# Scores of a local attention from fp16 parts scaled by a power of two, instead of rounded float32 parts; eight pairs in plain float32

## The chip, the core and the metric

The kernel runs on one core of one Trainium2 chip. The metric is the device time of one execution in microseconds (us), median of the runs. TensorE appears as PE (matmul) and PEld (weight load), VectorE as DVE, ScalarE as ACT, GpSimd as POOL; SP is the queue from which every transfer is issued.

## What is computed

There are 8 batches of 8 heads, 512 local positions, 32 global positions and a head dimension of 64. Every local query sees the keys within 32 positions and the 32 global keys; every global query sees all 544 keys. The result, joined over the heads to 4352 rows of 512, goes through a two-layer network with the activation h * tanh(softplus(h)).

```
s_g = scale * np.matmul(q_g, k_all.transpose(0, 1, 3, 2))
out_g = np.matmul(sm(s_g), v_all)
s_ll = np.where(mask, scale * np.matmul(q_l, k_l.T), -1e9)     # mask: |i - j| <= 32
s_lg = scale * np.matmul(q_l, k_g.transpose(0, 1, 3, 2))
out_l = np.matmul(sm(concat([s_lg, s_ll])), concat([v_g, v_l]))
h = x @ w_in
return (h * tanh(softplus(h))) @ w_out      # w_in 512 x 2048, w_out 2048 x 512
```

Queries and keys are drawn as normal numbers with spreads of 0.57 to 0.8. The weights arrive as 64-bit numbers and are turned into float32 bits on the chip.

## The kernel before

**Attention.** The unit is a pair of heads of one batch: 4 pairs in each of 8 batches, 32 pairs. A pair has 4 query tiles of 128 positions. For each tile and head `scores` (L594) makes the masked window of 192 or 224 scores, `row_max` (L611) the maximum on DVE, `expo` (L618) the exponentials on ACT, `p_hi` and `p_lo` (L636, L640) two fp16 parts, `p_turn` (L645) a transposing transfer of these (tile `pt`), and `pv` (L649) twelve small matmuls into `U`. `x_norm`, `x_split` and `x_turn` (L664 to L687) scale the result, part it and transpose it into `xh` and `xl`. The global queries go the same way through `g_scores` to `g_pv` (L690 to L751).

**How the scores are multiplied.** Most pairs use rounded float32 parts (type fp32r): `q_hi` and `k_hi` copy the raw tiles into `qs` and `ks`, `q_lo` and `k_lo` subtract to get the small parts (`kl`, and the upper 64 partitions of `qs`). The 128 rows of a matmul hold both parts of q, so that two matmuls, one on `ks` and one on `kl`, make one score tile: four matmuls in a tile of two heads. The first NPS = 5 pairs (`plain_s`: batch 0 and the first pair of batch 1) take float32 queries and keys as they are, 64 rows for each head, one matmul per head and tile (L601), which TensorE runs in two passes, so that the trace counts two. For g there are 12 matmuls in a pair: eight with 256 columns and four with 32.

**The network.** A step is a block of 256 rows and 256 of the 2048 inner columns: `m1_mm` (L779) makes `h` with two groups of 12 matmuls of 256 columns, `mish` (L828) the activation on ACT, `g_hi` and `g_lo` on DVE two fp16 parts `G`, and `m2_mm` (L848) adds two groups of 6 matmuls of 512 columns to `o`. There are 17 blocks of 8 steps; the last block holds the global rows. Block 0 needs `xh` and `xl` of all four pairs of batch 0, so the first `h` cannot stand before the fourth `x_turn`.

**Weights.** 32 halves of 512 KB are loaded (`w_load`); `w_bits` and `w_sum` (L380 to L395) build the float32 bits on DVE, ACT and POOL; `w_stat` (L397) sums squares on PE (`ws`), `w_norm` (L409) takes a scale from a sum over all partitions on POOL (`partition_all_reduce`), and `w_split` (L432) makes fp16 parts, with the low parts of the last ON_POOL = 3 of the first weight's eight column groups, and of all of the second weight, on POOL.

**What sets the order.** Every instruction is a task of `Plan` (L51) with an estimated duration. A list scheduler, run once while the kernel is built, simulates the five queues and emits the tasks in the order of their simulated starts; the engines then work their queues in that order. Priorities are the place in the code plus LATE_* amounts, or slots worked out from CONV1, RATE1, FIRST1 and the like (L1014 to L1028).

## Time and profile before

| | us |
|---|---|
| median of 3 runs | 1021.27 (1020.48 to 1023.16) |
| the profiled execution | 1018.93 |
| its span, first to last instruction | 1017.1 |
| first `h` matmul starts | 132.0 |
| last attention matmul done | 871.6 |

The share of busy time is an average over three stages: a start of 132 us in which batch 0's attention and the weights are made ready, a long middle in which attention and network are interleaved, and an end in which only the network is left. Idle time of an engine is put down to whatever released it last. Matmuls are pipelined, so that one takes longer from start to end than the next one waits; the chain of waits gives the time by which each group pushed the chain on.

### The profile page before, as it was taken

The numbers are of one execution on the slowest core, as the hardware profiler recorded it, in microseconds if no ns is written. First come the engines' busy times: TensorE is split into PE (matmuls) and PEld (weight loads), VectorE is DVE, ScalarE is ACT, GpSimd is POOL, SyncE is SP. The second block draws the span as 40 slices with busy tenths as digits, with TensorE's granted clock in tenths as the row PEclk, the third lists the DMA queues.
The fourth block names the chain that finished last, engine by engine and source line by source line (L and its number), as shares of the span: only waits on it lengthen the run. The fifth ranks groups of instructions, "written<-read, shape, count | busy, mean of one in ns | idle before, by whom it ended". The sixth has DMA issues, their size and how long they took to land.

```text
span 1017.1 us, 20581 instructions
## 1 busy us (share of the span) xinstructions
PE 925.7 (91%) x7906; PEld 664.6 (65%) x7906; DVE 668.5 (66%) x1704; ACT 680.9 (67%) x1321; POOL 82.2 (8%) x62
## 2 busy tenths in 40 slices
PE   3455696899999999999999999999999999999996
PEld 2233475566776777677777777777777777666663
DVE  6977796887766767776677666767676655322221
ACT  3465566777897788878878888788878888211110
POOL 3725231410000000000000000000000000000000
PEclk9997588999999999999999999999999999999999
DMA  9847982587758664766557665666676544100000
GB/s 333 228 111 175 262 259 63 112 180 189 168 104 180 144 143 113 177 148 143 123 153 161 134 133 129 155 135 141 117 165 127 123 81 77 42 1 22 1 22 21
DMA packets 231802, 134.65 MB, mean 132 GB/s; under 512 B 197528, under 2 KB 209048, under 8 KB 230680
## 3 DMA queue, kind: packets, MB, share of 16 engines
q1 hardware_dynamic: 231704, 133.34, 57.1%
q8 instruction: 62, 1.02, 0.4%
q14 instruction: 36, 0.29, 0.1%
HBM read 63.55 MB, written 8.91 MB: 71 GB/s over the span
## 4 chain that ended last, share of the span: by engine, by line
PE 65%; DVE 12%; DMA 8%; ACT 4%; issue 3%; SPq 1%; POOL 0%; ACTq 0%; DVEq 0%
PE o L856 28%; PE h L788 26%; PE s L608 4%; PE U L659 3%; DMA vraw<-in_vm 3%; DMA pt<-ph 2%; PE g L697 2%; DMA gpt<-gph 2%; PE gu L745 1%; DVE vmx L481 1%; DVE P L614 1%; DVE ph L642 1%; DVE G L309 1%; SPq L296 1%; DVE kl L546 1%
## 5 line engine op out<-in xcount | busy, mean ns | idle before, releaser
L856 PE MATMUL o<-W,G 128*128 128x512 f16 x1632 | 389.8, 379 | 0.3 <-POOL W L445 0.3
L788 PE MATMUL h<-xh,W 128*128 128x256 f16 x2048 | 379.0, 275 | 5.1 <-ACT e L831 5.1
L788 PEld LDWEIGHTS <-W 128*128 128x128 f16 x3264 | 311.2, 98 | 68.6 <-issue 5.3
L788 PE MATMUL h<-xl,W 128*128 128x256 f16 x1024 | 281.0, 274 | 0.0
L856 PEld LDWEIGHTS <-G 128*128 128x128 f16 x1632 | 156.9, 98 | 144.1 <-issue 0.6
L831 ACT ACTIVATE e<-h,c 128x512 f32<-128x512 f32 (+1 forms) x137 | 92.6, 683 | 117.5 <-PE h L788 116.6
L623 ACT ACTIVATE P<-P,nm 128x192 f32<-128x192 f32 (+1 forms) x256 | 117.8, 460 | 41.5 <-DVE nm L614 40.3
L309 DVE TENSOR_SCALAR G<-e,c 128x512 f16<-128x512 f32 x129 | 63.9, 495 | 118.5 <-ACT e L831 118.4
L614 DVE CUSTOM_DVE_ANT_0 P<-s,consts 128x192 f32<-128x192 f32 (+1 forms) x256 | 90.1, 367 | 68.1 <-PE s L608 57.7
L642 DVE SCALAR_TENSOR_TENSOR ph<-P,ph 128x384 f16<-128x384 f32 (+1 forms) x128 | 78.0, 611 | 80.1 <-ACT ph L307 79.3
L844 DVE SCALAR_TENSOR_TENSOR G<-e,c,G 128x512 f16<-128x512 f32 (+1 forms) x137 | 102.0, 745 | 3.4
L831 ACT ACT_TABLE_LOAD x79 | 101.4, 1283 | 1.4
L623 ACT ACT_TABLE_LOAD x74 | 94.9, 1283 | 1.3
L659 PEld LDWEIGHTS <-pt 96*128 96x128 f16 (+1 forms) x1536 | 59.3, 101 | 33.5 <-DMA pt<-ph 26.9
L307 ACT ACTIVATE ph<-P 128x384 f16<-128x384 f32 (+1 forms) x128 | 69.7, 548 | 16.3 <-DMA pt<-ph 13.2
L659 PE MATMUL U<-va,pt 128*128 128x64 f16 (+1 forms) x768 | 59.4, 199 | 19.7 <-DMA pt<-ph 19.7
L608 PE MATMUL s<-ks,qs 128*128 128x192 f32 (+1 forms) x216 | 71.4, 353 | 1.4 <-DVE qs L538 0.9
L659 PE MATMUL U<-vc,pt 96*128 96x64 f16 x768 | 58.7, 198 | 0.0
L718 ACT ACTIVATE gP<-g,gmx 64x288 f32<-64x288 f32 x64 | 30.4, 476 | 37.5 <-DVE gmx L713 37.4
L395 POOL TENSOR_TENSOR W<-W,wr 128x512 int32<-128x512 int32 x32 | 48.8, 1535 | 79.0 <-DVE W L393 40.1
L608 PE MATMUL s<-kl,qs 128*128 128x192 f32 (+1 forms) x216 | 54.2, 274 | 0.0
L405 PE MATMUL ws<-W 128*128 128x128 bf16 x128 | 17.7, 286 | 37.4 <-POOL W L395 37.3
(103 smaller groups left out, 1024.3 us busy)
## 6 DMA issues: line engine op xcount, KB each, us to landing
kraw<-in_kt SPq DMA_DIRECT2D x27, 640.0 KB, 4.7
qraw<-in_qt SPq DMA_DIRECT2D x27, 512.0 KB, 3.8
W<-in_w SPq DMA_DIRECT2D x19, 512.0 KB, 7.1
...
```

What stands on the lines that cost most here:

```text
L307: A.activation(out=dst, in_=src, func=AF.Copy, scale=c)
L309: V.tensor_scalar(dst, src, c, None, ALU.mult)
L395: pl.add(POOL, pool(512), lambda: G.tensor_tensor(f(), f(), X["wr", k], ALU.add), r=[("wr", k)], w=[key])
L608: T.matmul(X[s][:, :w], X[qs][:, h, t * 128:(t + 1) * 128], X[k][:, h, c0:c0 + w], start=(i == 0), stop=(i == 1))
L614: pl.add(DVE, 69 + 1.04 * w, lambda: V.tensor_tensor_reduce(out=X[P][:, h, :w], in0=X[s][:, :w], in1=mask[:, m0:m0 + w], scale=-SCALE, sca ...
L623: pl.add(ACT, 160 + 0.832 * w + 93, lambda: A.activation(out=X[P][:, h, :w], in_=X[P][:, h, :w], func=AF.Exp, bias=X[nm], scale=-1.0, accu ...
L642: pl.add(DVE, dve(n), lambda: V.scalar_tensor_tensor(p_part(X[ph], t, 1), p_src(X[P], t), PSC, p_part(X[ph], t, 0), ALU.mult, ALU.subtract ...
L659: T.matmul(X[u][:, t, h, :], X[pt][:k, p * 4 + h * 2 + c, :], X[vx][:k, t, vl, h * 64:(h + 1) * 64], start=(n == 0), stop=(n == 5))
L788: T.matmul(X[h][:, f * TB:(f + 1) * TB], wh(i, wl)[:, off:off + 128], X[x][:, d, o:o + TB], start=(n == 0), stop=(n == 11))
L831: chain(blk, i, ACT, 571, lambda a, z: A.activation(out=X[e][:, a:z], in_=hv(blk, i)[:, a:z], func=AF.Mish, bias=0.0, scale=X[c][:, 0:1]), ...
L844: chain(blk, i, DVE, 602, lambda a, z: V.scalar_tensor_tensor(gp(1, blk, i)[:, a:z], X[e][:, a:z], X["c", blk][:, 2:3], gp(0, blk, i)[:, a ...
L856: T.matmul(X[o], gp(g, blk, i)[:, f, t * 128:(t + 1) * 128], wh(8 + i, wl)[:, f * 512:(f + 1) * 512], start=(i == 0 and n == 0), stop=(i = ...
```

## The change

Eight pairs (batches 0 and 1) now take plain float32 (NPS = 8), in tiles of their own (`qn`, `kn`). For the 24 pairs of batches 2 to 7, queries and keys are first multiplied by powers of two, s and 1/s, which leaves the product as it is, and the parts are fp16. The factor of a batch comes from a new function, `b_norm`: four loads of 544 KB each bring all its queries and keys once more, laid out flat (`mxs`), a reduction of each on DVE takes the largest magnitude, POOL takes it over the partitions, and nine small DVE operations make s and 1/s (`sk`). `q_hi`, `q_lo`, `k_hi`, `k_lo` and `g_split` then multiply by `sk` as they convert. The raw-weight ring `wr` shrinks from two tiles to one, ON_POOL goes from 3 to 0, and the scheduler has new estimates (among them 4500 instead of 600 ns for the sum over partitions, and another model of the transfers) and new slots.

```diff
-NPS = 5
+NPS = 8
...
-          ("wr", 2, [128, 512], I32),
+          ("wr", 1, [128, 512], I32),
...
-          ("qs", 2, [128, 2, SL], F32R), ("ks", 2, [128, 2, KW], F32R), ("kl", 2, [128, 2, KW], F32R),
-          ("qgh", 2, [128, 3, HP, 64], F32R), ("vgf", 2, [128, 2, 128], F16),
+          ("qs", 2, [128, 2, SL], F16), ("ks", 2, [128, 2, KW], F16), ("kl", 2, [128, 2, KW], F16), ("qgh", 2, [128, 2, HP, 64], F16),
...
+          ("qn", 2, [128, 2, SL], F32), ("kn", 2, [128, 2, KW], F32), ("mx4", 1, [128, 4], F32), ("m4", 1, [128, 4], F32),
+          ("sk", 2, [128, 4], F32), ("vgf", 2, [128, 2, 128], F16),
...
-    ON_POOL = 3
+    ON_POOL = 0
...
+    def b_norm(b):
...
+        mx, m, sk = ("mx4", b), ("m4", b), ("sk", b)
+        for i in range(4):
+            k = ("kn", "m", b, i)
+            ring = "kraw" if b == 2 else "kn"
+            pl.add(DMA, dma(544), lambda i=i, k=k: load(X[k].rearrange("p a n -> p (a n)")[:, :1088], mxs[b, i]), new=[(ring, k)])
+            pl.add(DVE, dve(1088), lambda i=i, k=k: V.tensor_reduce(
+                out=X[mx][:, i:i + 1], in_=X[k].rearrange("p a n -> p (a n)")[:, :1088], axis=AX.X, op=ALU.max,
+                apply_absolute_value=True), r=[k], w=[[mx, i]] if i else (), new=() if i else [("mx4", mx)])
+        pl.add(DVE, 150, lambda: V.tensor_reduce(out=X[mx][:, 0:2], in_=X[mx].rearrange("p (a b) -> p a b", a=2), axis=AX.X,
+                                                 op=ALU.max), w=[mx])
+        pl.add(POOL, 4500, lambda: G.partition_all_reduce(X[m][:, 0:2], X[mx][:, 0:2], 128, RED.max), r=[mx], new=[("m4", m)])
...
+        def go():
+            a, s = X[m], X[sk]
+            V.tensor_scalar(a[:, 0:2], a[:, 0:2], TINY, None, ALU.max)
+            pow2(a[:, 0:2])
+            V.reciprocal(a[:, 2:3], a[:, 0:1])
+            V.tensor_tensor(a[:, 2:3], a[:, 2:3], a[:, 1:2], ALU.mult)
...
+            e = a[:, 2:3].bitcast(I32)
+            V.tensor_scalar(e, e, 1, None, ALU.logical_shift_right)
+            V.tensor_scalar(e, e, 0x20000000, None, ALU.add)
+            pow2(a[:, 2:3])
+            V.tensor_copy(s[:, 0:1], a[:, 2:3])
+            V.reciprocal(s[:, 1:2], a[:, 2:3])
+        pl.add(DVE, 1100, go, w=[m], new=[("sk", sk)])
...
-        q, rq = ("qgh", b), ("qgraw", b)
-        pl.add([(ACT, act(768)), (DVE, dve2(768))], 0, lambda e: copy(e, X[q], X[rq]), r=[rq], new=[("qgh", q)])
-        for a, h in ((1, HI), (2, LO)):
-            pl.add(DVE, dve(256), lambda a=a, h=h: V.tensor_tensor(X[q][h, a], X[rq][h, a], X[q][h, a].bitcast(F32), ALU.subtract),
-                   r=[rq], w=[[q, a]])
...
+        q, rq, sk = ("qgh", b), ("qgraw", b), ("sk", b)
+        pl.add([(ACT, act(512)), (DVE, dve2(512))], 0, lambda e: scaled(e, X[q], X[rq][:, 1:3], X[sk][:, 0:1]), r=[rq, sk], new=[("qgh", q)])
+        for a, h in ((0, HI), (1, LO)):
+            pl.add(DVE, dve(256), lambda a=a, h=h: V.scalar_tensor_tensor(X[q][h, a], X[rq][h, 1 + a], X[sk][h, 0:1], X[q][h, a], ALU.mult,
+                                                                          ALU.subtract), r=[rq, sk], w=[[q, a]])
...
-        pl.add(COPY(1024, b), 0, lambda e: copy(e, X[qs], X[q]), r=[q], new=[("qs", qs)])
+        pl.add(COPY(1024, b), 0, lambda e: scaled(e, X[qs], X[q], X["sk", b][:, 0:1]), r=[q, ("sk", b)], new=[("qs", qs)])
...
-        pl.add(DVE, dve(1024), lambda: V.tensor_tensor(X[qs][HI], X[q][HI], X[qs][HI].bitcast(F32), ALU.subtract), r=[q], w=[qs])
+        pl.add(DVE, dve(1024), lambda: V.scalar_tensor_tensor(X[qs][HI], X[q][HI], X["sk", b][HI, 0:1], X[qs][HI], ALU.mult, ALU.subtract),
+               r=[q, ("sk", b)], w=[qs])
...
-        pl.add(COPY(1280, b), 0, lambda e: copy(e, X[ks], X[k]), r=[k], new=[("ks", ks)])
+        pl.add(COPY(1280, b), 0, lambda e: scaled(e, X[ks], X[k], X["sk", b][:, 1:2]), r=[k, ("sk", b)], new=[("ks", ks)])
...
-        pl.add(DVE, dve(640), lambda: V.tensor_tensor(X[kl][:, h], X[k][:, h], X[ks][:, h].bitcast(F32), ALU.subtract),
-               r=[k, ks], w=[[kl, h]], new=() if h else [("kl", kl)])
+        pl.add(DVE, dve(640), lambda: V.scalar_tensor_tensor(X[kl][:, h], X[k][:, h], X["sk", b][:, 1:2], X[ks][:, h], ALU.mult, ALU.subtract),
+               r=[k, ks, ("sk", b)], w=[[kl, h]], new=() if h else [("kl", kl)])
...
-        pl.add(PE, mm(2, 262), go, r=[qs, ks, [kl, h]], new=[("sc", s)])
+        pl.add(PE, mm(2, 235), go, r=[qs, ks, [kl, h]], new=[("sc", s)])
...
-        pl.add(PE, mm(4, 262) + (1 - part) * 120, lambda: products([(X[q][:, 1 + h, hp, :], X[k][:, h]) for k in (ks, kl) for h in range(2)]),
+        pl.add(PE, mm(4, 262) + (1 - part) * 120, lambda: products([(X[q][:, h, hp, :], X[k][:, h]) for k in (ks, kl) for h in range(2)]),
...
-        if u == 11:
-            for n in range(HP, NPS):
-                plain_load(1, n - HP, "ks", kt0, KW)
-                plain_load(1, n - HP, "qs", qt0, SL)
+        if u in (8, 15):
+            for n in ((4, 5), (6, 7))[u == 15]:
+                plain_load(1, n - HP, "kn", kt0, KW)
+                plain_load(1, n - HP, "qn", qt0, SL)
...
-            g_split(b + 1)
...
+            if hp == (b > 1) and t == 2:
+                b_norm(b + 1)
...
+                if b > 1:
+                    g_split(b + 1)
+                b_split(b + 1)
+            if b == 1 and hp == 3 and t == 3:
+                b_load(b + 1, "g")
...
-    CONV1 = -1.0
+    CONV1 = 5.831
...
-    CONV2 = 8.279
+    CONV2 = 8.784
...
-    STEP1 = 0.114
-    FIRST2 = 14.027
+    STEP1 = 0.276
+    FIRST2 = 9.605
...
-    AHEAD_DMA = 3.119
-    LATE_K = 11.02
-    LATE_L = 158.572
-    LATE_B = 8.569
-    LATE_V = 0.0
+    LOAD1 = -2.202
+    LOADS1 = 0.213
+    AHEAD_DMA = 7.72
+    LATE_K = 33.326
+    LATE_L = 168.71
+    LATE_B = 9.983
+    LATE_V = 399.689
...
+            pl.slot = LOAD1 + LOADS1 * n
...
+            pl.slot = None
...
+    mxs = np.concatenate([np.concatenate([a.reshape(B, -1), g.reshape(B, -1)], axis=1) for a, g in ((q_l, q_g), (k_l, k_g))], axis=1)
+    mxs = mxs.reshape(B, 4, 128, 1088)
+    arrs = dict(qt=qt, kt=kt, qt0=qt0, kt0=kt0, mxs=mxs, vm=vm, vg=vg, qg=qg, **ws, consts=consts)
```

In the queue of transfers, near the fourth transposition into `xh` of batch 0 (`pt` and `gpt` are transposed probabilities, `W` and `wraw` loads of weights, `kraw` and `qraw` raw keys and queries, `in_mxs` the new loads). Before:

```order
L296 DMA W_70<-in_w2 128x1024 x2
L467 DMA_TRANSPOSE pt_0_3_3_1078<-ph1_73 128x8x128
L296 DMA W_70<-in_w2 128x1024
L467 DMA_TRANSPOSE gpt_0_3_1092<-gph0_80 128x10x64
L467 DMA_TRANSPOSE pt_1_0_0_1098<-ph0_72 128x8x128
L296 DMA W_70<-in_w2 128x1024
L296 DMA kraw_1_1_1128<-in_kt 128x1280
L467 DMA_TRANSPOSE xh_0_633<-xs_0_3_1125 128x4x128
L467 DMA_TRANSPOSE xl_0_638<-xs_0_3_1125 128x4x128
L296 DMA wraw_28_1167<-in_w2 128x1024
```

Now, at the same place:

```order
L300 DMA kn_m_2_3_1108<-in_mxs 128x1088
L471 DMA_TRANSPOSE gpt_0_3_1111<-gph0_80 128x10x64
L471 DMA_TRANSPOSE pt_0_3_3_1120<-ph1_73 128x8x128
L300 DMA kn_1_1_1057<-in_kt0 128x640
L300 DMA qn_1_1_1081<-in_qt0 128x512
L300 DMA wraw_30_1145<-in_w2 128x1024
L300 DMA W_70<-in_w2 128x1024
L471 DMA_TRANSPOSE pt_1_0_0_1167<-ph0_72 128x8x128
L300 DMA kraw_2_0_1185<-in_kt 128x1280
L300 DMA vraw_1_1210<-in_vm 128x2048
L471 DMA_TRANSPOSE xh_0_569<-xs_0_3_1215 128x4x128
L471 DMA_TRANSPOSE xl_0_577<-xs_0_3_1215 128x4x128
```

All 32 weight loads and the four `in_mxs` loads of batch 2 now stand ahead of the fourth `xh`; before, 28 weight loads did.

On DVE, at the scale of the second weight (`wd`, `wm`, `wp`, `iw`, `sw`; `G` are the network's first fp16 parts, named by block and step through `e`). Before:

```order
L412 ISA wd_1_1507,wm_1_1506<-ws_1_542,consts_65 128x128
L412 ISA wm_1_1506 128x1
L309 TENSOR_SCALAR G_2_1509<-e_0_4_1482,c_0_452 128x512
L844 SCALAR_TENSOR_TENSOR G_2_1509<-e_0_4_1482,c_0_452,G_2_1509 128x512
L417 TENSOR_SCALAR wp_1_1511<-wp_1_1511 128x1
L309 TENSOR_SCALAR G_2_1509<-e_0_5_1491,c_0_452 128x512
```

Now:

```order
L421 TENSOR_SCALAR wp_1_1290<-wp_1_1290 128x1
L313 TENSOR_SCALAR qs_2_1_1343<-qraw_2_1_1278,sk_2_1232 128x1024
L317 TENSOR_SCALAR wp_1_1290<-wp_1_1290 128x1
L320 TENSOR_SCALAR iw_67<-wp_1_1290 128x1
L321 RECIPROCAL sw_68<-iw_67 128x1
L429 TENSOR_SCALAR iww_69<-iw_67 128x1
L313 TENSOR_SCALAR ks_2_1_1362<-kraw_2_1_1306,sk_2_1232 128x1280
L313 TENSOR_SCALAR G_0_1385<-e_0_0_1367,c_0_683 128x512
```

The scale of the second weight moved from between the `G` of steps 4 and 5 to ahead of the first `G`.

## Rows read from the trace of the kernel before

**Rows 1.** page, part 2: 40 slices of 25.4 us, in tenths: PE busy, clock

```profile
PE   3455696899999999999999999999999999999996
PEclk9997588999999999999999999999999999999999
```

**Rows 2.** busy time by stretch: us, PE, PEld, DVE, ACT, POOL, clock, DMA share, GB/s

```profile
0.00:132.00 132.00, 70.61 (x460) 44.31 (x460) 104.24 (x241) 69.42 (x169) 54.81 (x42) 0.84 0.82 223
132.00:237.70 105.70, 91.48 (x799) 66.44 (x799) 88.43 (x207) 71.43 (x142) 25.62 (x15) 0.95 0.66 152
...
345.00:449.60 104.60, 103.55 (x943) 76.42 (x940) 74.22 (x201) 85.83 (x163) 0.35 (x1) 1.00 0.65 144
...
871.60:1017.10 145.50, 135.56 (x929) 90.28 (x925) 35.24 (x62) 24.28 (x37) 0.00 (x0) 0.98 0.05 17
```

**Rows 3.** chain of waits, 536 to 564 us: start us, us, what

```profile
538.54 0.52 PE s L608 x4
...
540.37 0.44 PE s L608 x4
...
543.79 2.59 PE o L856 x12
546.38 0.42 PE s L608 x4
546.80 0.37 PE U L659 x12
547.17 1.31 PE h L788 x12
548.49 1.17 PE g L697 x12
```

**Rows 4.** timeline of PE, 548 to 556 us: start us, us, instructions

```profile
553.50 0.27 PE L608 MATMUL s<-kl,qs 128*128 128x192 f32 x1
553.61 0.27 PE L608 MATMUL s<-ks,qs 128*128 128x192 f32 x1
...
553.84 0.26 PE L659 MATMUL U<-va,pt 128*128 128x64 f16 x3
```

**Rows 5.** waits over 1 us: PE 237.7 to 871.6 us, then DVE 250 to 870

```profile
PE U L659 <- DMA pt<-ph: 4.1, 6, 1.8
DVE vmx L481 <- DMA vraw<-in_vm: 11.2, 5, 3.3
```

**Rows 6.** timeline of PE, 127 to 142 us: plain scores and the first h

```profile
126.93 3.96 PE L601 MATMUL s<-ks,qs 64*128 64x224 f32 x12
130.82 1.27 PE L697 MATMUL g<-ks,qgraw 128*64 128x256 f32 x4
132.02 0.39 PE L788 MATMUL h<-xh,W 128*128 128x256 f16 x1
...
138.90 0.65 PE L697 MATMUL g<-ks,qgraw 128*64 128x256 f32 x2
```

**Rows 7.** groups by line and shape, whole span: busy us, mean ns, idle before

```profile
L546 DVE TENSOR_TENSOR kl<-kraw,ks 128x640 fp32r<-128x640 f32 x54 | 44.3, 821 | 0.2 <-ACT ks L300 0.2
L481 DVE TENSOR_REDUCE vmx<-vraw 128x1 f32<-128x512 f32 x32 | 20.6, 678 | 11.6 <-DMA vraw<-in_vm 11.6
L393 DVE SCALAR_TENSOR_TENSOR W<-W 128x512 int32<-128x512 int32 x19 | 20.7, 1091 | 0.1
L384 DVE TENSOR_SCALAR W<-W 128x512 int32<-128x512 int32 x19 | 12.6, 662 | 0.9 <-DMA W<-in_w 0.9
L440 DVE SCALAR_TENSOR_TENSOR W<-W,sw 128x1024 f16<-128x1024 f32 x5 | 6.7, 1336 | 0.9 <-ACT W L307 0.9
```

**Rows 8.** waits: DVE 0 to 135 us; DVE and PE 132 to 237.7: total, times, longest

```profile
DVE wp L417 <- POOL wp L416: 4.2, 1, 4.2
DVE wp L417 <- POOL wp L416: 4.6, 1, 4.6
PE h L788 <- ACT e L831: 5.1, 1, 5.1
```

49 lines of the change are left out of this document (25 added, 24 removed).

## The prediction

> **What bounds the kernel now.** I read the slices of the page first, then the busy times by stretch, the chain of waits in the middle, and the waits themselves. The slices [rows 1] show PE far from full for the first eight of 40 slices and at nine tenths from there to the end; its granted clock falls to half in slices 4 to 6. I cut the span at three marks: T1 = 132.0 us, where the first `h` matmul starts [rows 6]; T2 = 237.7 us, where 336 `h` and 144 `o` matmuls and all of batch 1's scores are issued; and 871.6 us, where attention ends. By the order these three marks fall at the same `h` count in both kernels, which is why I cut there.
>
> Up to T1 the bound is not PE (70.6 of 132 us busy) but DVE, 104.2 of 132, beside transfers with a share of 0.82 [rows 2]. Between T1 and T2 it is mixed: DVE 88.4 of 105.7 us, PE 91.5. From T2 to 871.6 us it is PE: in a batch of 104.6 us PE is busy 103.6, DVE 74.2, ACT 85.8 [rows 2], and PE's only wait of weight, for `pt`, is 4.1 us in six batches [rows 5]. After 871.6 us only the network is left and the change touches none of it.
>
> The chain gives what each group costs PE there [rows 3]: 12 `h` matmuls 1.31 us (109 ns each), 12 `o` 2.59 (216 ns), 12 `U` 0.37, 12 `g` 1.17, four score matmuls 0.42 to 0.52. Check for one batch: 32 x 1.31 + 16 x 2.59 + 16 x 0.37 + 4 x 0.45 (`gu`, an estimate from `U`) + 16 x 0.45 + 4 x 1.17 = 103.0 us, against 103.6 busy.
>
> **The change, part by part.**
>
> *Score matmuls in fp16, batches 2 to 7.* Two fp32r matmuls start 0.11 us apart with 192 columns [rows 4], and four with 224 columns take the same 0.44 [rows 3]: their pace is not that of the columns. For fp16 the price follows from two rows of the chain: 256 columns 109 ns and 512 columns 216 ns, so 0.418 ns a column and 2 ns; 192 columns 82 ns, 224 columns 96. That 128 x 128 fp16 weights come fast enough I take from `U`, 12 loads and 12 matmuls in 0.37 us, 31 ns a pair [rows 3]. A pair of heads has 8 matmuls of each width: 8 x 82 + 8 x 96 = 1.42 us against 2 x 0.42 + 0.44 + 0.52 = 1.80, so 0.38 less; 24 pairs make 9 us. Bounds: nothing, if the pace is kept, and 12 us.
>
> *g matmuls in fp16.* Eight of 256 columns stay at 109 ns; the four of 32 columns fall between 29 ns (the pace of `U`) and 58; 0.99 to 1.10 us against 1.17. I take 0.13 less, 3 us in 24 pairs; bounds 1.5 to 4.5. The Trainium skill (TensorE: Matmul & The Clock Gate, section on weight-path perf modes) says that the fast weight load is used for 128 weights that are not FP32. The weights of `g` are 64 wide, so by this rule its small matmuls would keep the slow load, 53 ns as an estimate from that page's P / 1.2; the sum would then lose 2.3 of the 3 us. No row of this trace has fp16 weights of 64 columns, so I leave the term as it is.
>
> *Three more plain pairs (batch 1).* Twelve tiles move from 0.45 us to plain float32. At half clock three plain tiles took 3.9 us [rows 6], 1.3 each. At full clock two g matmuls of 256 columns had 0.58 us until the next instruction where four, two of them small, took 1.2 at half clock [rows 6], so I halve: 0.65 a tile. That is 12 x 0.2 = 2.4 us more; `g` is even. Bounds: 0, where the two heads stand side by side, and 13 us, if all of it ran at half clock (12 x 0.85 + 3 x 1). The order sets eight of 24 heads alone among `h` and `o`, so the value lies above 0.
>
> *DVE and POOL, the largest values.* `mxs` is 24 reductions of 1088 elements; 512 take 678 ns [rows 7], so 1.4 us each, and ten small operations of 0.15 us a batch. Each of batches 3 to 7 gets 7 us: DVE goes from 74 to 81 of some 102 us, still under ACT's 86. PE hides it. What it does not hide is a wait in DVE's queue: the reductions of `vraw` wait for their load 2.2 us each time (11.2 us in five) [rows 5], and the five come with most of PE's 4.1 us. Queued behind such a wait are `row_max`, the `G` parts and `ph`, for which ACT, the transposition and PE wait. 20 loads of half that size after T2, at up to 0.45 us: 0 to 9 us, and I take 3. The conversions themselves change operation, from subtract to multiply-and-subtract; the nearest rows are 821 ns for 640 columns of the one and 1336 for 1024 of the other [rows 7], which is the same per column. I cost it at nothing.
>
> *The start, up to T1.* By the order, DVE does until the fourth `x_split` of batch 0: three more weight halves (0.66 + 1.09 us each [rows 7], 5.3 us), three low parts of the first weight that POOL did (1.34 each, 4.0 us), four reductions (5.6 us), three score tiles' maxima and some small work (2 us); it loses five reductions of values (3.4 us), `g_split` for batch 1 and two conversions (3 us). That is +10 us on 104. Against it, the 4.2 us for which DVE waits on POOL's sum over partitions [rows 8] now have work placed in them. Transfers: four more weight loads, `mxs` and others are 6 MB more before T1 on some 28 MB; at a share of 0.82 they still fit, with longer landings for what is queued behind. The smaller `wr` ring makes ACT wait for POOL in a chain that is not the last. I take T1 = 138; bounds 132 (DVE's idle 28 us absorb it) and 147 (they grow with the transfers).
>
> *From T1 to T2.* PE's work by the chain's prices is 28 x 1.31 + 12 x 2.59 + 13 x 0.37 + 3 x 0.45 + 12 x 0.45 + 3 x 1.17 = 83 us in 105.7, so 23 us are lost, among them 5.1 in one wait of `h` for ACT and 4.6 for the sum over partitions on DVE's side [rows 8]. In the change the second weight's scale stands ahead of the first `G` and the first `o` after 8 groups of `h` instead of 20; the float32 parts of batch 1 (4.5 us of DVE a pair) are gone, while two pairs of batch 2 take their place there earlier. The waits for `pt` stay. I take 13 us of loss, bounds 6 and 25. T2 = 138 + 83 + 2.4 + 13 = 236.4, 1.3 us earlier.
>
> *Sum.* On the span of 1017.1 us: -1.3 (start) - 9 - 3 + 3 = -10.3. The profiled execution took 1018.93, so 1008.6; the median of the runs lies 2.3 above that execution, so 1011 us.
>
> **The rivals.**
>
> *The start becomes shorter too.* T1 stays at 132 and the loss after it falls to 8: T2 = 225, 11 us more gain, 1000 us. For it: 28 us of DVE's idle time and the two waits on POOL. Against: DVE, PE and the transfers all get more to do before T2.
>
> *The scores keep their pace.* If something other than the weight load sets 0.11 us a matmul, the 9 us are gone: 1020 us, no change. `U` speaks against it.
>
> *Batch 1 runs at half clock.* Plain scores are the work PE did in the slices with the half clock [rows 1]. If it fell again between T1 and T2, the plain tiles cost 11 us more: 1022 us. Against: 480 `h` and `o` matmuls stand among them, and from T1 to T2 the mean clock was 0.95 [rows 2].
>
> *The reductions hold up DVE's queue: slower.* The place is an in-order engine that waits for a load while the scores' maxima stand behind. Before T1, where DVE is the bound and transfers are at 0.82, four loads at some 2.2 us each go straight onto T1, 9 us, and 20 later ones at 0.45 add 6 to what I took; with landings longer for the other transfers in the start, 5 more: 1031 us. It decides from about 0.45 us a load over what I took. For it: the load of `vraw` does just this [rows 5]. Against: the scheduler's new model of transfers sets the reductions later behind their loads, so that only what it misjudges is waited for.
>
> **How the numbers follow.** Forecast about 1011 (1001 to 1018 by its own bounds): 0.48. Shorter start, 1000: 0.19. Kept pace, 1020: 0.07. Half clock, 1022: 0.10. Held queue, 1031: 0.16. About 0.3%, 3 us, is what a measurement of this kernel can tell from no change. Faster by more than that: nearly all of the first two and a little of the third, 0.68. Within it: 0.15. Slower: 0.17, the held queue and a little of the half clock. The range from 996 to 1026 leaves out most of the held queue and the far end of the short start.
>
> **What would show it.** In the profile after: a group of four score matmuls in the chain at 0.33 to 0.39 us and a group of 12 `g` at 1.0 to 1.1; batches 3 to 7 at 102.6 us each against 104.6, with PE still busy for all but 1 us or so; waits of the new reduction for `in_mxs` well under 2 us each; the first `h` near 138 us and mark T2 near 236; plain tiles of batch 1 near 0.65 us with the clock at 1.0. The prediction is wrong in its main term if the batches stay at 104 us, and in its start if T2 lies under 228 or over 246.

## The result and the profile after

The changed kernel takes 1026.94 us (median of 18 runs, 1023.07 to 1030.62) against 1021.84 of the kernel before, measured beside it: ratio 1.0050, 95% interval 1.0038 to 1.0061. It is slower by half a per cent. I had forecast 1011 with a range of 996 to 1026, so the sign is wrong and the time lies just outside the range.

Its profiled execution took 1027.65 us with a span of 1025.7. At the marks of the prediction:

| us | before | forecast | after |
|---|---|---|---|
| T1, first `h` | 132.0 | 138 | 150.3 |
| T1 to T2 | 105.7 | 98.4 | 100.0 |
| T2 to the end of attention | 633.9 | 624.9 | 629.8 |
| the network's end | 145.5 | 145.5 | 145.6 |
| span | 1017.1 | 1006.8 | 1025.7 |

The stretch from T1 to T2 and the end came as forecast. Of the 18.9 us between forecast and result, 12.3 lie ahead of T1 and 4.9 after T2. The profiled execution of the kernel before lies 2.9 us below its median of 1021.84, that of the kernel after 0.7 above, so that the spans differ by 8.6 us where the medians differ by 5.1; in which stretch these 3.5 us lie no trace shows. The page's slices for the kernel after, answering to [rows 1], and its transfers:

```profile
PE   3444649899999999999999999999999999999996
PEclk8565559899999999999999999999999999999998
DMA  9977981577989976776677667666666643100000
```

The busy times by stretch, answering to [rows 2] (us, then PE, PEld, DVE, ACT, POOL, clock, DMA share, GB/s):

```profile
0.00:150.30 150.30, 67.02 (x484) 44.04 (x485) 111.70 (x265) 74.70 (x179) 55.30 (x44) 0.59 0.93 244
150.30:250.30 100.00, 94.54 (x771) 63.52 (x769) 72.74 (x179) 65.70 (x131) 18.84 (x11) 0.94 0.53 110
250.30:880.10 629.80, 619.12 (x5715) 442.68 (x5713) 469.15 (x1259) 510.29 (x975) 6.28 (x10) 1.00 0.70 153
459.00:566.00 107.00, 103.70 (x946) 73.75 (x943) 76.38 (x210) 86.09 (x163) 1.21 (x2) 0.98 0.71 141
```

And the one row of the kernel before that the third of these is to be set against:

```profile
237.70:871.60 633.90, 628.06 (x5728) 463.53 (x5727) 440.56 (x1197) 515.77 (x976) 1.75 (x5) 1.00 0.63 137
```

Up to T1 DVE has 111.7 us of work, 7.5 more than before and near the 114 of my sum; but it is idle for 39 us, where it was idle for 28. So work is not what made T1 late. After T2 PE's busy time fell by 8.9 us and its idle time rose from 5.8 to 10.7. And from the 720th `h` matmul on, four whole batches took no less than before; the rows of these stretches, before and after:

```profile
345.00:762.90 417.90, 414.40 (x3765) 306.05 (x3761) 297.03 (x808) 342.24 (x648) 1.40 (x4) 1.00 0.65 143
354.80:772.90 418.10, 409.62 (x3767) 292.66 (x3763) 310.84 (x846) 340.05 (x647) 3.44 (x6) 1.00 0.70 148
```

The 4.1 us that are gained after T2 lie in the batch ahead of that mark (107.3 to 104.5 us) and behind the last one.

**What T1 waits for.** PE's timeline shows the last thing ahead of the first `h` (start, us, instruction, idle before it and who ended that):

```profile
133.54 2.61 PE L638 MATMUL s<-kn,qn 64*128 64x224 f32 x8
147.89 0.61 PE L409 MATMUL ws<-W 128*128 128x128 bf16 x4 [11.74 <-POOL W L399]
```

PE is idle from 136.1 us, and what ends it is POOL, which adds the last weight bits. POOL's own timeline:

```profile
129.87 1.26 POOL L399 TENSOR_TENSOR W<-W,wr 128x512 int32<-128x512 int32 x1 [1.62 <-DVE W L397]
139.03 0.37 POOL L521 PARTITION_ALL_REDUCE m<-mx  x1 [7.89 <-issue]
146.59 1.25 POOL L399 TENSOR_TENSOR W<-W,wr 128x512 int32<-128x512 int32 x1 [7.19 <-DVE kl L583]
148.61 1.26 POOL L399 TENSOR_TENSOR W<-W,wr 128x512 int32<-128x512 int32 x1 [0.78 <-ACT wr L390]
```

The maximum over the partitions of batch 2, new in `b_norm`, stands ahead of the sums of the last two weight halves. It shows as 0.37 us, but POOL does nothing else from 131.1 to 146.6 us: 7.9 us before it and 7.2 after. The profile puts the 7.2 us down to a DVE instruction (`kl`), DVE's last event before the sum; but DVE's bits for this sum stood at 142.6 us, and two other ways back in this trace, put down to nothing, took 7.9 and 7.2 us (up to 80.21 and 163.63 us). POOL's queue has a pair of configuring instructions just ahead of the maximum and another, on the line of the sum, just behind it (lengths in ns, first and last start):

```profile
L521 POOLq MODIFY_POOL_CONFIG  x2: 9/9/9, 131.3 to 131.4; - x2
L399 POOLq MODIFY_POOL_CONFIG  x2: 82/82/83, 139.4 to 139.4; - x2
```

A part of the price falls on DVE, which waits for the maximum with the bits of these two halves behind it in its queue:

```profile
139.43 0.17 DVE L525 TENSOR_SCALAR m<-m 128x2 f32<-128x2 f32 x1 [2.62 <-POOL m L521]
141.87 0.69 DVE L397 SCALAR_TENSOR_TENSOR W<-wraw,W 128x512 int32<-128x512 int32 x1
```

So the sum comes 2.6 us later by DVE's wait and 4.0 us more by POOL's way back, 6.6 us in all. The same hole stood in the trace before, around the first weight's scale, and I had only read DVE's side of it [rows 8]:

```profile
50.10 1.51 POOL L395 TENSOR_TENSOR W<-W,wr 128x512 int32<-128x512 int32 x1 [0.69 <-DVE W L393]
57.51 0.40 POOL L416 PARTITION_ALL_REDUCE wp<-wm  x1 [5.89 <-issue]
66.41 3.10 POOL L395 TENSOR_TENSOR W<-W,wr 128x512 int32<-128x512 int32 x1 [8.50 <-ACT W L307]
```

The Trainium skill (GPSIMD Engine Reference, section on instruction dispatch) says that the first call of a freshly loaded kernel of that engine costs about 6 us that no instruction of the profile shows. The traces agree for the way in (5.8 to 7.9 us in the start of the two kernels) and show a second price of 7.2 to 7.9 us on the way back (8.5 in the last line, which is put down to ACT). Both are seen where the maximum or sum stands between other work of POOL. After T2, where POOL has no such work, the maximum starts 0.1 us after its input:

```profile
291.48 0.35 POOL L521 PARTITION_ALL_REDUCE m<-mx  x1 [24.89 <-DVE mx L519]
```

**What PE gained.** The chain of waits of the kernel after, 577 to 588 us, answering to [rows 3]:

```profile
577.80 0.38 PE s L645 x4
...
583.75 0.33 PE s L645 x4
...
585.75 1.12 PE g L734 x12
586.87 1.42 PE h L825 x12
```

and the piece that followed `g` in the kernel before:

```profile
549.66 1.33 PE h L788 x12
```

Four score matmuls take 0.33 us (192 columns) and 0.38 (224), as forecast: 1.42 us a pair against 1.80. `g` went from 1.17 to 1.12, but the `h` group behind it from 1.33 to 1.42: together 2.54 against 2.50, so `g` gained nothing. The 8.9 us of busy time hold a loss of some 1.7 us at half the clock (below); at full clock the work fell by some 10.6 us, where I had put 12.

**What PE lost.** PE's waits after T2, answering to [rows 5] (total, times, longest), then DVE's for loads:

```profile
PE gu L782 <- DMA gpt<-gph: 5.5, 7, 2.0
PE U L696 <- DMA pt<-ph: 3.2, 4, 1.4
```

```profile
DVE vmx L486 <- DMA vraw<-in_vm: 7.0, 4, 2.8
DVE mx L516 <- DMA kn_m<-in_mxs: 3.3, 3, 2.1
```

The reductions wait for their loads 3.3 us in all, and with those of the values it is 10.3 us, where the values alone had 11.2 before; so it isn't this wait that I had to fear. The order also has all 24 reductions done by 423 us, so they load no batch behind that. The longest wait for `gpt` has a second price. PE's timeline:

```profile
490.30 0.27 PE L825 MATMUL h<-xh,W 128*128 128x256 f16 x1
492.58 0.32 PE L782 MATMUL gu<-gpt,va 128*128 128x64 f16 x3 [2.01 <-DMA gpt<-gph]
492.70 0.83 PE L782 MATMUL gu<-gpt,vf 128*128 128x64 f16 x12
493.34 2.75 PE L893 MATMUL o<-W,G 128*128 128x512 f16 x6
...
554.33 1.46 PE L893 MATMUL o<-W,G 128*128 128x512 f16 x6
```

and the granted clock of that stretch:

```profile
492.50:496.00 3.50, 3.42 (x22) 1.74 (x22) 0.75 (x1) 2.38 (x4) 0.00 (x0) 0.51 0.75 178
```

After 2.0 us of idleness PE works at 1.2 GHz until 496 us: six `o` matmuls take 2.75 us, which take 1.46 at 2.4 GHz. By half of these 3.5 us the batch loses some 1.7 us more than the wait, and it takes 107.0 us where its neighbours take 104.2 and 101.8. Such a stretch does not follow every wait of this length: in e2 below PE waits 2.2 us at the same place and works on at full clock.

```profile
483.15 0.25 PE L782 MATMUL gu<-gpt,va 128*128 128x64 f16 x3 [2.16 <-DMA gpt<-gph]
```

```profile
483.10:486.60 3.50, 3.45 (x38) 2.61 (x38) 1.44 (x6) 2.75 (x5) 0.00 (x0) 1.00 0.84 176
```

### The profile page after: what moved, and what is told of

It is laid out like the page before. It is cut to its first block, busy times and chain, and to the rows that moved or that the text cites. A ratio compares the mean times of both kernels' runs of the same rounds, so it can differ in the third digit from the quotient of the medians.

```text
span 1025.7 us, 20580 instructions
## 1 busy us (share of the span) xinstructions
PE 916.3 (89%) x7888; PEld 640.6 (62%) x7888; DVE 688.9 (67%) x1763; ACT 674.6 (66%) x1319; POOL 80.4 (8%) x65
## 4 chain that ended last, share of the span: by engine, by line
PE 64%; DVE 15%; DMA 8%; ACT 5%; issue 4%; POOL 2%; SPq 1%; POOLq 0%; DVEq 0%; ACTq 0%
PE o L893 26%; PE h L825 26%; DMA gpt<-gph 4%; PE U L696 3%; PE s L645 3%; POOL W L399 2%; PE g L734 2%; DMA vraw<-in_vm 2%; PE s L638 2%; DVE kl L583 2%; DVE G L881 1%; PE gu L782 1%; DMA pt<-ph 1%; DVE W L397 1%; DVE P L651 1%
## 5 line engine op out<-in xcount | busy, mean ns | idle before, releaser
L893 PEld LDWEIGHTS <-G 128*128 128x128 f16 x1632 | 158.6, 98 | 150.3 <-issue 6.3
L313 DVE TENSOR_SCALAR G<-e,c 128x512 f16<-128x512 f32 (+1 forms) x128 | 62.8, 490 | 117.7 <-ACT e L868 117.2
L881 DVE SCALAR_TENSOR_TENSOR G<-e,c,G 128x512 f16<-128x512 f32 (+1 forms) x137 | 105.5, 770 | 3.8 <-ACT G L311 0.8
L696 PEld LDWEIGHTS <-pt 96*128 96x128 f16 (+1 forms) x1536 | 64.7, 101 | 20.2 <-issue 8.3
L409 PEld LDWEIGHTS <-W 128*128 128x128 bf16 x128 | 10.7, 125 | 79.4 <-POOL W L399 78.4
L638 PE MATMUL s<-kn,qn 64*128 64x192 f32 (+1 forms) x128 | 38.6, 521 | 10.9 <-DVE nm L651 6.2
```

Of the source, the lines that this page charges most:

```text
L313: V.tensor_scalar(dst, src, c, None, ALU.mult)
L638: pl.add(PE, mm(1, 4 * w), lambda: T.matmul(X[s][:, :w], X[q][r, part, t * 128:(t + 1) * 128], X[k][r, part, c0:c0 + w], start=True, stop= ...
L696: T.matmul(X[u][:, t, h, :], X[pt][:k, p * 4 + h * 2 + c, :], X[vx][:k, t, vl, h * 64:(h + 1) * 64], start=(n == 0), stop=(n == 5))
L881: chain(blk, i, DVE, 602, lambda a, z: V.scalar_tensor_tensor(gp(1, blk, i)[:, a:z], X[e][:, a:z], X["c", blk][:, 2:3], gp(0, blk, i)[:, a ...
L893: T.matmul(X[o], gp(g, blk, i)[:, f, t * 128:(t + 1) * 128], wh(8 + i, wl)[:, f * 512:(f + 1) * 512], start=(i == 0 and n == 0), stop=(i = ...
```

## The experiments

All medians are measured beside the kernel before; I compare ratios to it, whose intervals are about 0.2% (2 us) to either side. The three marks on the right come from one profiled execution each, which can lie 3 to 4 us off its kernel's median (e1 3.7 below, e13 3.0 above), so that a few us between two traces show nothing by themselves. "Kept order" means that every queue has the same instructions in the same order, but for those that the edit names.

| run | ratio | 95% interval | T1 | `h` 720 | T2 to the end of attention |
|---|---|---|---|---|---|
| before | 1 | | 132.0 | 345.0 | 633.9 |
| after | 1.0050 | 1.0038 to 1.0061 | 150.3 | 354.8 | 629.8 |
| e1 no maximum on POOL | 0.9973 | 0.9955 to 0.9991 | 141.7 | 347.1 | 626.7 |
| e14 and small reductions | 0.9952 | 0.9934 to 0.9970 | 141.4 | 344.6 | 627.1 |
| e2 and small loads | 0.9944 | 0.9921 to 0.9968 | 144.3 | 346.5 | 625.2 |
| e8 and two `wr` | 0.9932 | 0.9907 to 0.9957 | 140.7 | 343.2 | 623.1 |
| e3 after, two `wr` | 1.0012 | 0.9995 to 1.0028 | 147.7 | 353.6 | 628.3 |
| e5 maximum later | 1.0073 | 1.0052 to 1.0094 | 141.5 | 356.4 | 625.6 |
| e6 e5, two `wr` | 1.0041 | 1.0027 to 1.0055 | 139.6 | 355.4 | 624.3 |
| e9 maximum on DVE | 1.0127 | 1.0104 to 1.0150 | 146.6 | 356.9 | 638.0 |
| e10 e9, two `wr` | 1.0100 | 1.0082 to 1.0117 | 142.7 | 352.3 | 638.6 |
| e11 all four on DVE | 1.0161 | 1.0139 to 1.0182 | 137.4 | 352.9 | 645.7 |
| e7 before in fp16 | 0.9960 | 0.9945 to 0.9975 | 131.7 | 342.6 | 631.3 |
| e15 e7 planned anew | 0.9922 | 0.9902 to 0.9941 | 131.8 | 344.3 | 630.1 |
| e4 no factor, planned anew | 1.0109 | 1.0083 to 1.0135 | 151.6 | 361.6 | 630.5 |
| e12 planner told | 1.0032 | 1.0014 to 1.0050 | 135.9 | 355.1 | 642.1 |
| e13 a factor a row | 0.9979 | 0.9963 to 0.9996 | 142.2 | 351.3 | 629.8 |

("`h` 720" is the time of the 720th `h` matmul; it is a fairer mark than T2 where the order differs.)

### The factor's price, piece by piece in the kept order

The maximum over the partitions alone (e1):

```diff
-        pl.add(POOL, 4500, lambda: G.partition_all_reduce(X[m][:, 0:2], X[mx][:, 0:2], 128, RED.max), ...
+        pl.add(POOL, 4500, lambda: G.tensor_copy(X[m][:, 0:2], X[mx][:, 0:2]), ...
```

> Changed kernel, every queue in the same order; only the six maxima over the partitions in b_norm are left out: POOL copies its 2 numbers instead, so that each partition takes its own power of two. Theory A (POOL's queue): the start is late because the maximum over partitions of batch 2 and POOL's return from it held POOL from 131.1 to 146.6 us, with the sums of the last two weight halves, their ws matmuls and so the first h behind it. Then the first h falls from 150.3 to 138 to 142 us, where the fourth transposition into xh lands, and the time by 8 to 12 us, to about 1017. Theory B (more DVE work and more transfers in the start): POOL's hole is cover only, the first h stays at 147 to 150 us and the time above 1024. From the first h of mark T2 to the end of attention both expect 630 us within 2, as now, since POOL stands idle there.

It took 1019.75 us, ratio 0.9973: some 7 to 8 us of the change's price are this one kind of instruction, just under theory A's 8 to 12. POOL's timeline in this run:

```profile
127.57 1.26 POOL L399 TENSOR_TENSOR W<-W,wr 128x512 int32<-128x512 int32 x1 [1.62 <-DVE W L397]
128.88 0.18 POOL L521 COPY m<-mx 128x2 f32<-128x2 f32 x1
137.68 1.52 POOL L399 TENSOR_TENSOR W<-W,wr 128x512 int32<-128x512 int32 x1 [8.62 <-DVE W L397]
```

The copy takes 0.18 us, and the next sum now waits for DVE's bits. The first `h` comes at 141.7 us, as theory A had it. The sum ahead of the copy already began 2.3 us earlier than in the changed kernel, so of the 8.6 us only 6 to 7 are the maximum's: from that sum to the next it is 10.1 us here, and also in e14, e2 and e8, where the changed kernel has 16.7. After T2 I had expected no change, and the trace has 3.1 us less; 1.7 of these are the stretch at half clock, which this trace doesn't have, and the rest is within what one execution differs from another.

Then small reductions with whole loads (e14), and small loads as well (e2):

```diff
-                out=X[mx][:, i:i + 1], in_=X[k].rearrange("p a n -> p (a n)")[:, :1088], axis=AX.X, op=ALU.max,
+                out=X[mx][:, i:i + 1], in_=X[k].rearrange("p a n -> p (a n)")[:, :16], axis=AX.X, op=ALU.max,
...
-            ... load(X[k].rearrange("p a n -> p (a n)")[:, :1088], mxs[b, i]), ...
+            ... load(X[k].rearrange("p a n -> p (a n)")[:, :16], mxs[b, i][:, :16]), ...
```

For e14:

> As the run with POOL's copies in place of the maxima over the partitions, with the 24 loads of mxs whole, but each reduction on DVE takes 16 of the 1088 columns; what is left out is that DVE time, 1.2 us each. It splits the 3.7 us between that run (1019.75) and the one with small loads and small reductions (1016.0). If DVE's time is what counts: 1016 to 1017. If the transfers are: 1019 to 1020.

For e2:

> As the run without the maximum over the partitions, and besides each of the 24 loads of mxs brings 16 of its 1088 columns and each reduction takes 16: nearly all of b_norm's transfers (13 MB) and DVE time are left out, the order of every queue is kept. Theory A: the start gains at most 3 us more over the run with POOL's copies alone, since its last wait is POOL's; and if the waits of U and gu for their transposed probabilities (8.7 us in the changed kernel, 5.4 before) come from the 20 loads after T2, the 629.8 us from T2 to the end of attention fall to 624 to 626. Rival (those waits come from where the order puts the transpositions, not from the loads): 629 to 630 us stay. Theory B for the start: the first h falls only here, to about 138 us.

Ratios 0.9952 and 0.9944: loads and reductions cost some 3 us together. The medians put 2 of these on DVE's time and 1 on the transfers, as e14's expectation had it for the first case; but each step is of the size of the intervals, so the split is not shown. In the traces e14's gain lies ahead of `h` 720, where 19 of the 24 reductions stand; from there to the end of attention e1 took 521.4 us and e14 522.9. e2's first `h` comes 2.6 us later than e1's, though it has less to do; why is open. PE's idle time after T2 fell from 10.7 us to 9.4 (e1), 9.7 (e14) and 8.4 (e2), not to the 5.8 of before: half or more of the waits that were added stay without `b_norm`'s costs.

### The single `wr` tile

```diff
-                    pool.tile(shape, dt, tag=tag, name=name, bufs=bufs))
+                    pool.tile(shape, dt, tag=tag, name=name, bufs=2 if tag == "wr" else bufs))
```

(The planner still counts one, so the order is kept.)

For e3:

> Changed kernel in the same order of every queue, with two raw-weight tiles wr instead of one. Theory A (the maximum over partitions of batch 2 sets the first h): the sums of the first weight run closer together, its scale comes up to 10 us earlier than 71.9 us, but the first h stays at 146 to 151 us and the time within 4 us of 1027. Rival C (the single tile, in a chain of ACT and POOL that repeats every 2.04 us or more, delays everything in the start): the first h falls by 6 to 10 us, the time to 1017 to 1021.

For e8:

> Changed kernel in the same order of every queue, with all three prices of the factor and the ring taken out: POOL copies instead of the six maxima over the partitions, 16 of 1088 columns of mxs, and two tiles wr. What is left against the kernel before is the arithmetic, three more plain pairs and the new order. If the prices add (1016.0 without the factor's costs, 3.3 for the ring): 1012 to 1014, first h at 140 to 142. If the ring's price was only what stood ahead of the maximum: 1015 to 1017, first h at 143 to 145.

Two tiles took 0.38% off the changed kernel (e3), with T1 at 147.7 us: within what A allowed, but not the nothing that I had put down for the ring. Without the factor's costs they took 0.12% (e8 against e2, within the intervals), and 0.3% in each of the two other pairs (e6 against e5, e10 against e9). The pairs agree in sign; I put it at 1 to 4 us. The first ten sums show how (POOL, e3):

```profile
25.62 16.12 POOL L399 TENSOR_TENSOR W<-W,wr 128x512 int32<-128x512 int32 x10 [11.48 <-DVE W L388]
```

Ten sums in 16.1 us, where the changed kernel needs 22.6 (from 24.83 to the end of the tenth at 47.46): there ACT can only write `wr` again when POOL has read it. The first weight's scale, which I expected up to 10 us earlier, gained only 1.8 (70.11 against 71.92 us). Where POOL's hole meets the single tile, ACT stands too: at the first weight's scale, in the changed kernel, it waits 8.5 us for POOL to read the tile, with its own conversions behind, and DVE waits 9.1 us for one of those.

```profile
81.49 0.66 ACT L390 ACTIVATE wr<-wraw 128x512 int32<-128x512 uint32 x1 [8.51 <-POOL W L399]
```

With two tiles DVE's wait is gone, but it waits 7.3 us for PE's `g` instead. And at the end of the start, above, the last sum waits for ACT's `wr` and this for the sum before it: that is the chain to the first `h`. e8 holds the arithmetic, the three plain pairs and the new order without the factor's and the ring's price: 0.9932, so that these prices are 1.2% or 12 us together. Its time of 1014.15 is at the edge of what I expected if they add. Its PE row after T2:

```profile
240.80:863.90 623.10, 617.00 (x5716) 442.12 (x5714) 449.26 (x1259) 510.55 (x975) 5.06 (x10) 1.00 0.65 138
```

Here alone PE's idle time (6.1 us) is near that of before, and the five batches from T2 on take 102.4, 102.6, 104.3, 102.2 and 104.5 us, 9.2 us less than before, where 102.6 us each would have made it some 12. But this execution lies 2.8 us below its kernel's median, and e2, which has 8.4 us of idle time, differs from it only in a tile that is last used ahead of T2; so how much of this is e8's own is open.

### Moving the maximum, and telling the planner

e5 lets the maximum of batch 2 wait for the second weight's sums, so that POOL runs it in one group with two others; e6 adds the second tile; e12 gives the planner 7.0 us for each of them and 7.2 after it.

```diff
-        ... 128, RED.max), r=[mx], new=[("m4", m)])
+        ... 128, RED.max), r=[mx] + [("wm", 1)] * (b == 2), new=[("m4", m)])
```

For e5:

> Changed kernel, complete, with one edge more for the planner: the maximum over the partitions of batch 2 waits for the second weight's sums, so that it stands on POOL behind the last sum of weight bits, in one group with the two others of the start. Theory A (POOL held for 15 us ahead of the last two sums sets the first h): the first h comes at 141 to 144 us, as where that maximum was left out (141.7 and 144.3), mark T2 at 242 to 245, the time at 1018 to 1021. Rival: batch 2's conversions, which need the factor and now come some 15 us later, or the longer group of maxima ahead of the second weight's low parts, delay the stretch from T1 to T2 from 100 to 106 us or more; then the time stays at 1024 to 1028.

For e6:

> As the run with the later maximum, in its order of every queue, with two raw-weight tiles wr instead of one. The second tile alone took 3.3 us off the changed kernel. If the two waits lie one behind the other on the way to the first h, it takes 2 to 4 us off here too: first h at 138 to 141 us, time 1014 to 1018. If the second tile helped only by shortening what stood ahead of the maximum over the partitions, nothing is left of it here: the time is the other run's within 1 us.

For e12:

> Changed kernel, complete, planned anew with 7.0 us for each maximum or sum over the partitions and POOL taken for 7.2 us more after it, in place of 4.5 us, as the trace shows them. If a misjudged time put the maximum of batch 2 in the wrong place and a planner that knows it does better: first h at 138 to 145 us, T2 at 240 to 246, the time 1016 to 1022. Rival (the other constants are fitted to the old estimate, and a new order loses elsewhere what it wins there, as the two other newly planned runs did with 1028.6 and 1033.7): 1025 to 1035.

In e5 T1 is where theory A wants it, 141.5 us, and the time is no better (1.0073): the rival was right on what follows. From T1 to T2 it takes 112.9 us. PE's longest wait there and ACT's queue:

```profile
PE h L825 <- ACT e L868: 8.8, 1, 8.8
```

```profile
159.16 1.04 ACT L304 CAST W<-W 128x1024 f16<-128x1024 f32 x1 [2.49 <-POOL W L449]
...
162.61 1.26 ACT L868 ACTIVATE e<-h,c 128x512 f32<-128x512 f32 x2
```

In the new order ACT's conversions of the second weight stand ahead of the first activations, and one of them waits for POOL, which comes back to its low parts only at 157.0 us. POOL's hole has a new place, and PE waits for it there. e6 has its first `h` where I expected it, at 139.6 us, but it stands on e5's order and misses the 1014 to 1018 us. e12 reaches T1 at 135.9 us, but its 720th `h` comes at 355.1, as in the changed kernel, and it ends at 1.0032, between both theories: not clear of the changed kernel's 1.0050, and not faster than before.

### The maximum on DVE

e9 makes the maximum with two transpositions of 32 x 32 blocks, two reductions and some copies of a few elements inside `b_norm`'s small operations (`mx4` has two buffers there); e11 makes the sums and maxima of the weights and values this way too. The core of e9's edit, with `sq` a tile of its own:

```diff
+            V.tensor_copy(sq[:, 0, 0:2], X[mx][:, 0:2])
+            V.transpose(sq[:, 1], sq[:, 0])
+            V.tensor_reduce(out=sq[:, 2, 0:1], in_=sq[:, 1], axis=AX.X, op=ALU.max)
+            for i in range(4):
+                V.tensor_copy(sq[0:32, 3, i:i + 1], sq[32 * i:32 * i + 32, 2, 0:1])
+            V.tensor_reduce(out=sq[0:32, 2, 1:2], in_=sq[0:32, 3, 0:4], axis=AX.X, op=ALU.max)
+            V.tensor_copy(sq[0:32, 1], sq[0:32, 2, 1:2].broadcast_to([32, 32]))
+            V.transpose(sq[0:32, 3], sq[0:32, 1])
+            for i in range(4):
+                V.tensor_copy(a[32 * i:32 * i + 32, 0:2], sq[0:32, 3, 0:2])
```

For e9:

> Changed kernel, complete, every queue in the same order, but the maximum over the partitions in b_norm is made on DVE inside its small-operations task (two 32 x 32 transpositions, two reductions, nine copies of a few elements, an estimate of 13 x 0.15 = 2 us a batch) instead of on POOL. Theory A (what costs is POOL's 15 us, not the work of the maximum): the run without the maxima gave 1019.75; 2 us of DVE work in the start, ahead of the last two weight halves, come on top, so first h at 143 to 147 us and the time 1019 to 1023. Rival (any maximum over the partitions at this place of the order holds up the start by its latency): the time stays at 1025 or more.

For e10:

> As the run with the maximum on DVE, with two raw-weight tiles wr, in the same order. By the other runs the second tile gives 1.9 to 3.7 us: 1016 to 1020, which would be a complete version faster than both kernels by 2 us or more. If DVE's small operations take the ring's gain away, 1020 to 1023.

For e11:

> As the run with the maximum on DVE and two wr tiles, and the sums over the partitions for the two weights' scales and the maxima for the values' scales are made on DVE in the same way, so that POOL runs nothing but its additions and low parts; same order of every queue. Theory A, extended: POOL stood still for 15 us around the first weight's scale as well (65.1 to 80.2 us in the changed kernel), and 13 to 15 us around the second's, with sums and low parts behind; then the first h comes at 130 to 137 us and the time falls below the other run's by 4 to 10 us, to 1008 to 1014. Rival (DVE and transfers bound the start once POOL's hole of batch 2 is gone): within 3 us of the other run.

I was wrong in all three times. The start did what A says: T1 146.6 us (e9), 142.7 (e10), 137.4 (e11, without any hole on POOL). But after T2 e9 takes 638.0 us, 8.2 more than the changed kernel, and e11 645.7. PE's waits there (e9):

```profile
PE gu L793 <- DMA gpt<-gph: 11.8, 10, 2.0
```

The new operations take 2.23 us of DVE a batch, in one block, 11.2 us for the five batches after T2. With that work in an engine that is busy for three quarters of the time the stretch is 8.2 us longer; 6.3 us of it are PE's waits for `gph`'s transposition (11.8 against 5.5 us). That an engine has idle time doesn't mean that a block of 2 us in its queue is hidden.

### The arithmetic alone

e7 is the kernel before with fp16 parts in the halves of the same tiles, without a factor, order kept; e15 has besides the shorter estimate of a score task (the last two lines), which gives a new order.

```diff
+    half = lambda k: X[k].bitcast(F16)[..., :X[k].shape[-1]]
...
-        pl.add(COPY(1280, b), 0, lambda e: copy(e, X[ks], X[k]), r=[k], new=[("ks", ks)])
+        pl.add(COPY(1280, b), 0, lambda e: copy(e, half(ks), X[k]), r=[k], new=[("ks", ks)])
...
-        pl.add(PE, mm(2, 262), go, r=[qs, ks, [kl, h]], new=[("sc", s)])
+        pl.add(PE, mm(2, 235), go, r=[qs, ks, [kl, h]], new=[("sc", s)])
```

For e7:

> The kernel before, the order of DVE, ACT, POOL, SP and of PE's matmuls kept, with the score parts of its 27 pairs in fp16 instead of rounded float32, in the halves of the same tiles; there is no factor (1 for every batch) and five pairs in plain float32 as before. This is the arithmetic of the change alone. From my terms: 27 pairs by 0.38 us (s) and 0.05 to 0.13 (g, by the blocks measured in the changed kernel) make 11.6 to 13.8 us of PE's work; 24 of the pairs lie in the stretch that PE bounds, where 10 to 12 us are taken off 633.9. Theory A (the change's arithmetic is worth what I forecast, its loss comes from the factor and the new order): time 1009 to 1013, first h at 132, T2 236 to 238, then 622 to 625. Rival (PE's gain turns into waits for the transposed probabilities, which come no earlier): the stretch after T2 takes 628 to 632, the time 1016 to 1020.

For e15:

> The kernel before with the score parts in fp16 without a factor, as in the run that gave 1017.45, but planned anew with one number changed, the estimate of a score task of two matmuls, 218 to 196 ns. In the old order PE's busy time after T2 fell by 7.8 us and its idle time rose by 5.2. If that rise came from transpositions that the order issues too late for a faster PE, the new order lets the gain through: after T2 624 to 627 us, time 1011 to 1014. If any new order costs what it happens to cost (the others gave 1023.9 to 1033.7), the time lies on either side, 1013 to 1025, and waits of another kind than pt and gpt show up.

e7 gives 0.9960, 4 us, where I expected 10 to 12; the rival named this. Its row after T2 and PE's waits:

```profile
236.50:867.80 631.30, 620.30 (x5729) 442.35 (x5727) 440.30 (x1197) 515.69 (x976) 1.76 (x5) 1.00 0.63 137
```

```profile
PE U L659 <- DMA pt<-ph: 7.1, 6, 2.3
PE gu L745 <- DMA gpt<-gph: 3.2, 5, 1.1
```

PE's busy time fell by 7.8 us and its idle time rose by 5.2, from 5.8 to 11.0: the transposed probabilities come no earlier, and PE, which is done sooner, waits for them. One of these waits, 2.3 us at 520 us, is followed by 3.4 us at a granted clock of 0.50. e15 has the same work in another order and takes 8 us off (0.9922), the lowest median of all, though e8's interval reaches it. Its trace doesn't show why: this profiled execution (1015.86 us) lies 2.3 us above its median, still has 7.8 us of waits for `pt`, and has two such stretches of 3.4 us at half clock (from 312.3 and 626.4 us), while e7's (1015.25) lies 2.2 below its median. That the order decides is shown by the medians; by which wait is open.

### No factor, planned anew; a factor for each row

For e4, where `b_norm(b + 1)` is replaced by a fill with ones:

> Changed kernel with b_norm left out as a whole (the factor is 1 for every batch), planned anew, so that the queues' orders differ too. If the fp16 parts are worth 12 us after T2 as I forecast, with nothing of b_norm's price, the batches take 102.6 us each, attention after T2 some 622 us; with the first h at 132 to 140 us the time is 1000 to 1010. Theory A wants the first h at most at 141. If the fp16 parts are worth less (PE's busy time fell by 8.9 us from T2 on, not 12), attention after T2 takes 625 to 627 and the time is 1008 to 1014.

For e13:

```diff
-        pl.add(POOL, 4500, lambda: G.partition_all_reduce(X[m][:, 0:2], X[mx][:, 0:2], 128, RED.max), ...
+        pl.add(POOL, 4500, lambda: (G.tensor_copy(X[m][0:64, 0:2], X[mx][64:128, 0:2]), G.tensor_copy(X[m][64:128, 0:2], X[mx][0:64, 0:2])), ...
...
-            V.tensor_scalar(a[:, 0:2], a[:, 0:2], TINY, None, ALU.max)
+            V.scalar_tensor_tensor(a[:, 0:2], a[:, 0:2], TINY, X[mx][:, 0:2], ALU.max, ALU.max)
```

> Changed kernel, every queue in the same order, without any maximum over the partitions: mxs is laid out so that a partition holds the values of one position of the head dimension, each such row takes its own power of two (the product stays the same, since q and k of one row take s and 1/s), the two halves of the partitions are joined by two small copies on POOL and one DVE operation that takes the place of another. Two tiles wr. Nothing that the reference wants is left out. From the runs without the maxima (1019.75) and with the second tile (1.9 to 3.3 us): first h at 138 to 142 us, h number 720 at 343 to 346 us, time 1016 to 1018.5, faster than both kernels. Rival (DVE's queue is so tight that only leaving work out helps, as 2.2 us more a batch cost 8 us after T2): 1020 to 1023.

e4 leaves out `b_norm`, as e2 does but for its smallest pieces, and lets the planner make a new order: 1.0109 against 0.9944, 17 us that only the new order can have cost. Batch 2's conversions, no longer held by the factor, stand in DVE's queue ahead of the last weights, T1 is 151.6 us, and behind it `h` waits 11.2 us for ACT. So it says nothing of the factor's price; e2 does.

e13 gives each position of the head dimension a factor of its own, so that nothing has to go over the partitions (`mxs` is laid out for it, and `mx4` has two buffers), and has two `wr` tiles. It leaves nothing out. 1020.49 us, ratio 0.9979 (0.9963 to 0.9996): faster than the changed kernel by 0.7% and than the kernel before by 0.2%. It is 2 to 4 us short of what I expected, in the rival's range; why is open. T1 (142.2) is as expected, but `h` 720 comes at 351.3 us instead of 343 to 346, and the stretch to T2 takes 104.0 us in this execution, which lies 3.0 us above its median.

## Why the prediction was wrong

By its own steps:

- **The score matmuls** were right: 1.42 us a pair, in the chain to the hundredth, 9 us of PE's work.
- **The `g` matmuls** were mis-sized: 3 us forecast, none measured, since 0.09 us went to the `h` group behind each and only 0.05 came from `g`. My lower bound of 1.5 us was too high. The rule of the Trainium skill (TensorE: Matmul & The Clock Gate, section on weight-path perf modes) that I weighed there would have left 0.7 of the 3 us; the trace, which now has fp16 weights of 64 columns, is nearer to it than to my term.
- **Three more plain pairs** were mis-sized: at full clock a tile of 192 columns takes 0.53 us in the chain where its two heads stand side by side (four records), less than my 0.65, but a head alone (two records) takes 0.52 as well. The 12 tiles between T1 and T2 took 9.7 us in all, 0.81 each, so 4.3 us more and not 2.4; some 0.9 of it is one group at half clock. The half clock in batch 1, a rival, didn't come as a whole: the clock from T1 to T2 was 0.94.

```profile
198.55 0.53 PE s L638 x4
...
200.67 0.52 PE s L638 x2
```

- **The reductions in steady state** (+3 us, priced by the wait for loads): the size is about right (some 3 us with the loads, e2 against e1), the mechanism is not shown. DVE's waits for loads did not grow, and there is no steady state, since the order has the reductions done by 423 us. That the time they hold DVE is what counts is likely, by e14 and by e9 with 11.2 us of work for 8.2 us of time, but e14's step is not clear of the intervals.
- **The gain after T2** failed in a step that the prediction takes without a reason: that PE's shorter work ends as shorter time. The batches from `h` 720 on took 104.2, 107.0, 101.8 and 105.1 us, as long as before and not 102.6, which is the prediction's own sign that its main term is wrong, though the score groups have the forecast price; in the old order more than half of it became waits for `pt` and `gpt` (e7). Of the 4.9 us short of the forecast some 1.4 are PE's work, 1.7 the half clock, and 1.9 idle time of PE beyond the 3 us that I had put down.
- **T1** is where most was lost, and T2 at 250.3 us is over the 246 that the prediction named for a wrong start. "The smaller `wr` ring makes ACT wait for POOL in a chain that is not the last" was wrong by 1 to 4 us (e3, e6, e8, e10). And a sum or maximum over the partitions was priced as a wait of DVE that could be filled with work [rows 8]; what is queued behind it on POOL, the sums of the last two weight halves and with them `ws` and the first `h`, was not named. That cost 6 to 7 us at T1 and 0.77% of the time (e1); 2.6 us of it came by DVE's wait, which was not filled, and 4.0 by POOL's way back.
- **T1 to T2**, 98.4 forecast and 100.0 measured, and the end were right; the 1.6 us are about what the plain pairs took more.

The rival that ended on the slow side, a held queue with 1031 us, had the sign and nearly the size, but that is luck, since its place is wrong: the queue that was held is POOL's first, and DVE's only through it, by an instruction and not by a load. I gave it 0.16.
